# Batch 0 of a gated attention and mixer kernel: z loaded as f32, doubled on VectorE and turned on TensorE

## The chip, the cores and the metric

The kernel runs on one core of a Trainium2 chip. The metric is the device time in microseconds (us) of one execution; the median of several executions is compared. A core has five engines with a queue of instructions each: TensorE (PE in the profile, its weight loads PEld), VectorE (DVE), ScalarE (ACT), GpSimd (POOL) and SyncE (SP). DMA transfers are issued from POOL's queue and from SP's queue here. An instruction that waits holds up everything behind it in its own queue.

## The reference

Two layers, one behind the other, over 8 batches of 3008 rows. The inputs u and v are 8 x 3008 x 256, z is 8 x 3008 x 64, all f32.

```python
scores = (1.0 / S) * np.matmul(z, z.transpose(0, 2, 1))
attn = np.maximum(scores, 0.0) ** 2
x = u * np.matmul(attn, v)                       # gated attention
xt = x.transpose(0, 2, 1)
h = np.maximum(xt @ w_tok1, 0.0) @ w_tok2        # 3008 -> 256 -> 3008
y = x + h.transpose(0, 2, 1)
h2 = np.maximum(y @ w_ch1, 0.0) @ w_ch2          # 256 -> 1536 -> 256
return y + h2
```

## The kernel before

Rows are taken in 24 tiles of 128 (the last has 64 rows, held twice, in both halves of the partitions), four tiles to a **group** of 512 keys. A batch has six rows of groups, one for each block q of 512 queries, and in each row six groups g of 512 keys. `groups` (L179) lists all 288 in the order in which they are worked on; `key_order` (L165) gives the keys of the first row as 0, 5, 1, 2, 3, 4. In batch 0 every group is computed directly; in later batches the ones below the diagonal come from transposing those above it by DMA (`fl`, L213 to L216).

The program's order is written by hand. The loop at L452 takes the groups one by one, and in each: the fetches that `at_group` (L405) has put at this group's number; then `scores` of the group one ahead; then `av` of this group, in two halves of 128 channels; between the halves, from batch 1 on, pieces of the mixer of the batch before (`mix`, L442).

- `scores` (L182): four matmuls with 64 rows of contraction on zT, two at a time in the two halves of the array. For this z is held twice, side by side, so that its transpose fills 128 partitions. They write two PSUM tiles of two banks each (tag `ps`, three buffers for everything that uses the tag). ACT takes each through a scaled ReLU to `rl` (L204), DVE squares it into `at` (L208, L210).
- `av` (L222): eight matmuls on v and `at` into two accumulators of one bank each (tags `acc0`, `acc1`, one buffer each).
- `gate` (L260): at the end of a row of groups DVE multiplies an accumulator by uT into `xT` (L270, L275); after the second one a DMA transpose on SP makes `x` for the mixer (L279).

The steps around the change: `load_z` (L80) loads z on POOL and converts it to bf16 in the DMA (tag `zs`); `turn_z` (L90) doubles it to `zr` (tag `zr`, two buffers) with a copy on the engine that it is given, and transposes it by DMA on SP into zT (L95). `load_v` (L98) loads v on POOL, with conversion. `load_uT` (L108) loads u on POOL with conversion (tag `ur`, two buffers; L111, L114) and right behind it in the program transposes it by DMA on SP (L116; tag `uT`, three buffers). `load_w_tok1`, `load_w_tok2` (its staging tile has tag `ws`, one buffer) and `load_w_ch` bring the weights on POOL.

Before the loop (L393 to L400) the kernel asks, key group by key group, for z and v of batch 0, and after the third for uT(0, 0). Then it doubles and turns the first z with DVE (L439) and computes its scores. In the first five passes of the loop the z of the next group is doubled on DVE and turned on SP (L457 to L459), right ahead of its scores. uT(0, 1) is asked for at group 4, later ones two rows of groups ahead, at the third group of a row (L413). The z of later batches is doubled on POOL (L424).

Of the kernel before, what the change touches and what calls it, by code (L numbers as in the profile page):

```python
# [6 lines left out]

F32 = mybir.dt.float32
BF16 = mybir.dt.bfloat16
# [3 lines left out]
P = 128  # L13
QW = 512
GK = 4
# [12 lines left out]
def kernel(  # L28
# [11 lines left out]
    nc = tc.nc  # L40
    B, S, D = u.shape
    d_qk = z.shape[-1]
# [3 lines left out]
    TAIL = S - (KT - 1) * P  # L46
# [4 lines left out]
    NQ = (S + QW - 1) // QW  # L51
    NG = KT // GK
# [3 lines left out]
    consts = ctx.enter_context(tc.tile_pool(name="consts", bufs=1))  # L56
    sb = ctx.enter_context(tc.tile_pool(name="sb", bufs=2))
    psum = ctx.enter_context(tc.tile_pool(name="psum", bufs=2, space=bass.MemoryType.PSUM))
# [3 lines left out]
    w_tok2_sb = consts.tile([P, DT, S], BF16)  # L62
    w_ch1_sb = consts.tile([P, DT, d_ch], BF16)
    w_ch2_sb = consts.tile([P, CHT, D], BF16)

# [2 lines left out]
    full_tiles = [w // P for w in widths]  # L70

    def rows_of(ap, c):

        n = full_tiles[c]
        return ap[c * QW:c * QW + n * P, :].rearrange("(p t) d -> p t d", t=n)

    def last_rows(ap):
        return ap[(KT - 1) * P:, :]

    def load_z(b, c):  # L80
        zs = sb.tile([P, GK, d_qk], BF16, tag="zs", name="zs", bufs=6)
        n = full_tiles[c]
        nc.gpsimd.dma_start(out=zs[:, :n, :], in_=rows_of(z[b], c))
        if n < GK:
            for r in range(2):
                nc.gpsimd.dma_start(
                    out=zs[r * TAIL:(r + 1) * TAIL, n, :], in_=last_rows(z[b]))
        return zs

    def turn_z(zs, zT, c, engine):  # L90


        zr = sb.tile([P, GK, 2, d_qk], BF16, tag="zr", name="zr", bufs=2)
        engine.tensor_copy(zr[:], zs.unsqueeze(2).to_broadcast([P, GK, 2, d_qk]))  # L94
        nc.sync.dma_start_transpose(  # L95
            out=zT[:, c * GK:c * GK + GK, :], in_=zr.rearrange("p t h d -> p (t h d)"))

    def load_v(b, c):  # L98
        vt = sb.tile([P, GK, D], BF16, tag="v", name="v_sb", bufs=8)
        n = full_tiles[c]  # L100
        nc.gpsimd.dma_start(out=vt[:, :n, :], in_=rows_of(v[b], c))  # L101
        if n < GK:
            for r in range(2):
                nc.gpsimd.dma_start(
                    out=vt[r * TAIL:(r + 1) * TAIL, n, :], in_=last_rows(v[b]))
        vs[b, c] = vt

    def load_uT(b, q):  # L108
        ur = sb.tile([P, QW // P, D], BF16, tag="ur", name="ur", bufs=2)
        n = full_tiles[q]  # L110
        nc.gpsimd.dma_start(out=ur[:, :n, :], in_=rows_of(u[b], q))  # L111
        if n < QW // P:
            nc.gpsimd.memset(ur[TAIL:, n, :], 0.0)
            nc.gpsimd.dma_start(out=ur[:TAIL, n, :], in_=last_rows(u[b]))  # L114
        uT = sb.tile([P, QW // P, DT, P], BF16, tag="uT", name="uT", bufs=3)
        nc.sync.dma_start_transpose(  # L116
            out=uT.rearrange("p t h s -> p (t h) s"),
            in_=ur.rearrange("p t d -> p (t d)"))
        uTs[b, q] = uT
# [35 lines left out]

    zTs, vs, uTs, xTs, xs = {}, {}, {}, {}, {}
    attn = {}

    def direct_block(b, q, g):

        return b == 0 or g >= q

    def key_order(b, q):  # L165
        direct = [g for g in range(NG) if direct_block(b, q, g)]
        if q == 0:
            return [direct[0], direct[-1]] + direct[1:-1]
        direct = [direct[-1]] + direct[:-1]
        flipped = [g for g in range(NG) if not direct_block(b, q, g)]  # L170
        order = []
        while direct or flipped:
            if direct:
                order.append(direct.pop(0))
            if flipped:
                order.append(flipped.pop(0))
        return order

    groups = [(b, q, g) for b in range(B) for q in range(NQ) for g in key_order(b, q)]  # L179
    directs = [t for t in groups if direct_block(*t)]  # L180

    def scores(b, q, g):  # L182
        zT = zTs[b].rearrange("p t s -> p (t s)")
        W = widths[q]
        pss = []
        for pr in range(GK // 2):
            sc = psum.tile([P, 2, QW], F32, tag="ps", name="sc", bufs=3)
            for r in range(2):
                k = g * GK + pr * 2 + r
                h = slice(r * d_qk, (r + 1) * d_qk)  # L190
                nc.tensor.matmul(  # L191
                    sc[:, r, :W], zT[h, k * P:(k + 1) * P], zT[h, q * QW:q * QW + W],
                    start=True, stop=True)
            pss.append(sc)
        at = sb.tile([P, GK * QW], BF16, tag="at", name="at", bufs=3)
        flip = g > q and b > 0
        if flip:

            a4 = at.rearrange("p (j i s) -> p j i s", i=GK, s=P)
        else:  # L200
            a3 = at.rearrange("p (i w) -> p i w", w=QW)
        for pr, sc in enumerate(pss):
            rl = sb.tile([P, 2, QW], BF16, tag="rl", name="rl", bufs=3)
            nc.scalar.activation(rl[:, :, :W], sc[:, :, :W], ACT.Relu, scale=inv_S)  # L204
            pair = slice(2 * pr, 2 * pr + 2)
            if flip:
                r4 = rl.rearrange("p i (j s) -> p j i s", s=P)
                nc.vector.tensor_mul(a4[:, :, pair, :], r4, r4)  # L208
            else:
                nc.vector.tensor_mul(a3[:, pair, :W], rl[:, :, :W], rl[:, :, :W])  # L210
        if flip:
            attn[b, q, g] = a4.rearrange("p j i s -> p i j s")
            fl = sb.tile([P, GK, QW], BF16, tag="fl", name="fl", bufs=10)  # L213
            nc.sync.dma_start_transpose(
                out=fl.rearrange("p j (i s) -> p (j i) s", s=P), in_=at[:])
            attn[b, g, q] = fl[:, :, :]  # L216
        else:
            attn[b, q, g] = a3
# [171 lines left out]
    def new_zT(b):  # L390
        zTs[b] = sb.tile([P, KT, P], BF16, tag="zT", name="zT", bufs=2)

    vorder = key_order(0, 0)  # L393
    new_zT(0)
    zs0 = {}
    for j, c in enumerate(vorder):
        zs0[c] = load_z(0, c)
        load_v(0, c)
        if j == 2:
            load_uT(0, 0)  # L400


    fetch = {}
# [1 line left out]
    def at_group(n, f):  # L405
        fetch.setdefault(n, []).append(f)

    for b in range(B):
        base = b * NQ * NG
        for q in range(NQ):  # L410
            m = b * NQ + q + 2
            if m < B * NQ:
                at_group(base + q * NG + 2, lambda m=m: load_uT(m // NQ, m % NQ))  # L413
        if b + 1 < B:
            held = {}

            def ask_z(b, c, held):
                held[c] = load_z(b + 1, c)

            at_group(base + 3 * NG, lambda b=b: new_zT(b + 1))  # L420
            for j, c in enumerate(vorder):
                at_group(base + 3 * NG + j, lambda b=b, c=c, h=held: ask_z(b, c, h))
                at_group(base + 3 * NG + j + 3, lambda b=b, c=c, h=held:
                         turn_z(h.pop(c), zTs[b + 1], c, nc.gpsimd))  # L424
                at_group(base + (NQ - 1) * NG - 2 + (j if j > 1 else 0),
                         lambda b=b, c=c: load_v(b + 1, c))
    at_group(4, lambda: load_uT(0, 1))
    for c in range(NG):
        at_group(NG + 1 + 4 * c, lambda c=c: load_w_tok1(c))
        at_group(NG + 3 + 4 * c, lambda c=c: load_w_tok2(c))  # L430
# [5 lines left out]
    flat = NQ * NG * 1.73 + NQ * (NQ + 1) / 2 * 0.63  # L436
    budget = 0.0
    ahead = 1
    turn_z(zs0[vorder[0]], zTs[0], vorder[0], nc.vector)  # L439
    scores(*directs[0])  # L440

    def mix(n, left):  # L442
        nonlocal budget
# [8 lines left out]
    for n, (b, q, g) in enumerate(groups):  # L452
        for f in fetch.get(n, []):
            f()
        first, last = n % NG == 0, n % NG == NG - 1
        t = 1.73
        if n + 1 < NG:  # L457
            c = groups[n + 1][2]
            turn_z(zs0[c], zTs[0], c, nc.vector)  # L459
        if direct_block(b, q, g) and ahead < len(directs):  # L460
            scores(*directs[ahead])
            ahead += 1
            t += 0.63
        if b >= 1:
            budget += per_batch * t / flat
        got = budget
        pre, half = av(b, q, g, first, last)
        for f in pre:
            f()
        if not last:  # L470
            half(0)
            mix(n, got / 2)
            half(1)
            mix(n, 0.0)
        else:
            half(0)
            gate(b, q, 0)
            half(1)
            gate(b, q, 1)
            mix(n, 0.0)  # L480
        if q == NQ - 1 and last:
            head, tail = mixer(b, n + 3)
            queue = head + queue + tail
# [32 lines left out]
```

## Time and profile before

| what | value |
|---|---|
| median of 3 runs | 1269.73 us (1267.84 to 1270.58) |
| the profiled execution | 1268.72 us |
| its span, first to last instruction | 1267.0 us |
| mean granted clock of TensorE in it | 0.992 |
| busy: PE, DVE, ACT, POOL | 1192.7, 603.9, 499.9, 147.9 us |

The profile's groups of instructions give line, engine, operation, output and inputs, shapes, then the count, the busy time in us, the mean of one in ns, and behind the second bar the idle time of the engine just before them and what ended it. In the timeline and the chain of waits the first number is the start and the second the duration, both in us from the start of the span. A DMA issue shows on POOL or on SPq, the queue of SyncE; its duration there is that of the issue, not of the transfer.

In the profile's 40 slices of the span, 31.7 us each, the share of PE's time that is busy is a digit in tenths, and so is the granted clock:

```profile
PE   1399999999999999999999999999999999999998
PEclk9799999999999999999999999999999999999999
```

### The profile page before, as it was taken

The page shows a single profiled execution, that of the slowest core. Times are in us where ns is not written, and L with a number is a line of the kernel's source. Part 1 is how long each engine was busy: PE and PEld are TensorE (multiplying, and loading weights), DVE is VectorE, ACT ScalarE, POOL GpSimd, SP SyncE. Part 2 cuts the span into 40 slices and gives each one's busy share as a digit, 9 for nine tenths or more (in the row PEclk, how much of TensorE's full clock was granted, in tenths as well). Part 3 has the DMA queues.
Part 4 walks back from the last instruction along what each step waited for, and adds up shares of the span by engine and source line. Part 5 has one row for each costly group of instructions (what it writes and reads, how often), then busy time and mean ns, then how long its engine had stood idle before and what let it go on. Part 6 is the DMA issues. An engine that isn't in the chain of part 4 may idle for free.

```text
span 1267.0 us, 17239 instructions
## 1 busy us (share of the span) xinstructions
PE 1192.7 (94%) x6986; PEld 623.6 (49%) x7068; DVE 603.9 (48%) x780; ACT 499.9 (39%) x519; POOL 147.9 (12%) x277
## 2 busy tenths in 40 slices
PE   1399999999999999999999999999999999999998
PEld 0133444555455645455455554555455554555565
DVE  1156565444644355534644436543564446444443
ACT  1267644334343144433444343432443334442122
POOL 3323220011101110011200111002110110000000
PEclk9799999999999999999999999999999999999999
DMA  7656995679658697679956797577966788563122
GB/s 112 104 80 95 165 157 117 133 124 177 119 119 144 127 159 125 117 135 154 153 115 109 137 161 138 108 142 132 171 119 129 128 133 155 109 116 83 32 76 65
DMA packets 439487, 157.59 MB, mean 124 GB/s; under 512 B 403504, under 2 KB 417008, under 8 KB 439408
## 3 DMA queue, kind: packets, MB, share of 16 engines
q1 hardware_dynamic: 411040, 123.78, 51.1%
q0 software_dynamic: 28368, 32.72, 18.4%
q8 instruction: 55, 0.90, 0.3%
q14 instruction: 24, 0.20, 0.1%
HBM read 65.40 MB, written 24.64 MB: 71 GB/s over the span
## 4 chain that ended last, share of the span: by engine, by line
PE 83%; DVE 6%; DMA 4%; issue 3%; ACT 2%; POOL 0%; DVEq 0%; ACTq 0%; POOLq 0%
PE acc L244 36%; PE op L351 20%; PE hp L333 17%; PE sc L191 7%; PE a_ps L298 3%; DVE xT L316 3%; ACT rl L204 2%; DMA zT<-zr 2%; DVE h2pre L338 1%; DVE xT L270 1%; DVE at L208 1%; DMA ur<-in_u_dram 1%; DMA fl<-at 1%; DMA uT<-ur 1%; PE h_ps L312 0%
## 5 line engine op out<-in xcount | busy, mean ns | idle before, releaser
L204 ACT ACTIVATE rl<-sc 128x1024 bf16<-128x1024 f32 (+1 forms) x366 | 351.8, 1014 | 424.3 <-PE sc L191 424.3
L244 PE MATMUL acc<-at,v_sb 128*128 128x512 bf16 (+2 forms) x1450 | 361.7, 382 | 14.9 <-DVE xT L270 11.8
L244 PEld LDWEIGHTS <-v_sb 128*128 128x128 bf16 (+1 forms) x2304 | 208.6, 98 | 294.1 <-issue 99.6
L351 PE MATMUL op<-w_ch_sb,h2pre 128*128 128x256 bf16 (+1 forms) x2304 | 279.1, 273 | 1.1
L333 PE MATMUL hp<-xT,w_ch_sb 128*128 128x512 bf16 (+1 forms) x1120 | 272.0, 374 | 2.7 <-DVE xT L316 0.2
L340 ACT ACTIVATE h2pre<-hp 128x1024 bf16<-128x1024 f32 (+1 forms) x144 | 144.9, 1006 | 281.6 <-PE hp L333 263.9
L351 PEld LDWEIGHTS <-h2pre 128*128 128x128 bf16 (+1 forms) x2304 | 224.3, 98 | 62.1 <-ACT h2pre L340 6.3
L208 DVE TENSOR_TENSOR at<-rl 128x1024 bf16<-128x1024 bf16 x210 | 147.7, 705 | 188.3 <-ACT rl L204 188.2
L338 DVE TENSOR_SCALAR h2pre<-hp 128x1024 bf16<-128x1024 f32 (+1 forms) x144 | 172.5, 1200 | 79.3 <-PE hp L333 79.3
L244 PE MATMUL acc<-fl,v_sb 128*128 128x512 bf16 (+1 forms) x805 | 197.3, 370 | 1.8
L333 PEld LDWEIGHTS <-w_ch_sb 128*128 128x128 bf16 x1152 | 112.7, 98 | 131.4 <-issue 4.4
L210 DVE TENSOR_TENSOR at<-rl 128x1024 bf16<-128x1024 bf16 (+1 forms) x156 | 107.7, 699 | 143.1 <-ACT rl L204 139.3
L191 PE MATMUL sc<-zT 64*128 64x512 bf16 (+1 forms) x732 | 114.8, 386 | 47.8 <-DMA zT<-zr 45.7
L359 DVE TENSOR_TENSOR res<-op,u_sb 128x512 f32<-128x512 f32 x88 | 60.6, 689 | 156.3 <-PE op L351 156.3
L270 DVE TENSOR_TENSOR xT<-acc,uT 128x512 bf16<-128x512 f32 (+1 forms) x96 | 61.6, 664 | 62.3 <-PE acc L244 61.8
L94 POOL COPY zr<-zs 128x512 bf16<-128x512 bf16 x42 | 28.8, 685 | 494.6 <-DMA zT<-zr 494.3
L191 PEld LDWEIGHTS <-zT 64*128 64x128 bf16 x732 | 22.2, 94 | 118.1 <-issue 69.5
L316 DVE TENSOR_TENSOR xT<-xT,h_ps 128x1024 bf16<-128x1024 bf16 (+1 forms) x48 | 53.9, 1193 | 19.5 <-PE h_ps L312 19.5
L111 POOL DMA_DIRECT2D ur<-in_u_dram x48 | 25.9, 541 | 246.2 <-DMA uT<-ur 244.1
L312 PE MATMUL h_ps<-w_tok_sb,a_sb 128*128 128x512 bf16 (+1 forms) x191 | 43.4, 374 | 1.7 <-ACT a_sb L304 0.7
L298 PE MATMUL a_ps<-x_sb,w_tok_sb 128*128 128x256 bf16 x384 | 44.4, 273 | 0.0
L101 POOL DMA_DIRECT2D v_sb<-in_v_dram x48 | 26.0, 543 | 144.2 <-PE acc L244 143.4
(25 smaller groups left out, 145.4 us busy)
## 6 DMA issues: line engine op xcount, KB each, us to landing
out_dram<-res SPq DMA_DIRECT2D x88, 256.0 KB, 2.2
v_sb<-in_v_dram POOLq DMA_DIRECT2D x40, 256.0 KB, 4.3
ur<-in_u_dram POOLq DMA_DIRECT2D x40, 256.0 KB, 5.1
zs<-in_z_dram POOLq DMA_DIRECT2D x40, 64.0 KB, 2.9
fl<-at SPq DMA_TRANSPOSE x105, 4.4
v_sb<-in_v_dram POOLq DMA_DIRECT2D x8, 192.0 KB, 5.7
w_ch_sb<-in_moe_w_ch_dram POOLq DMA_DIRECT2D x4, 384.0 KB, 5.8
ur<-in_u_dram POOLq DMA_DIRECT2D x8, 192.0 KB, 3.3
```

What stands on the lines that cost most here:

```text
L191: nc.tensor.matmul(sc[:, r, :W], zT[h, k * P:(k + 1) * P], zT[h, q * QW:q * QW + W], start=True, stop=True)
L204: nc.scalar.activation(rl[:, :, :W], sc[:, :, :W], ACT.Relu, scale=inv_S)
L208: nc.vector.tensor_mul(a4[:, :, pair, :], r4, r4)
L210: nc.vector.tensor_mul(a3[:, pair, :W], rl[:, :, :W], rl[:, :, :W])
L244: nc.tensor.matmul(o, vt[rows, i, dh * P:(dh + 1) * P], rhs, start=st, stop=sp, skip_group_check=True)
L270: nc.vector.tensor_mul(xT[:, dh, :full * P].rearrange("p (t s) -> p t s", s=P), acc[:, :full * P].rearrange("p (t s) -> p t s", s=P), uT[: ...
L298: nc.tensor.matmul(st["a_ps"][:, th, :], w_tok1_sb[:, k, th * P:(th + 1) * P], x[:, :, i, :], start=(k == 0 and th == 0), stop=(k == KT - ...
L316: nc.vector.tensor_add(xT[:, :, :W], xT[:, :, :W], h[:, :, :W])
L333: nc.tensor.matmul(hp[:, r, :W], w_ch1_sb[:, dc, cc * P:(cc + 1) * P], xT[:, dc, :W], start=(dc == 0), stop=(dc == DT - 1))
L338: nc.vector.tensor_single_scalar(h2[:, :, :W], hp[:, :, :W], 0.0, AX.max)
L340: nc.scalar.activation(h2[:, :, :W], hp[:, :, :W], ACT.Relu)
L351: nc.tensor.matmul(op[:rows[i], i, :], st["h2", q, cc // 2][:, cc % 2, c0:c0 + rows[i]], w_ch2_sb[:, cc, :], start=(cc == 0 and i == 0), s ...
```

## The change

For batch 0, z is loaded without conversion, as f32, on SP (`first_z`; its tile shares tag `x`). DVE doubles all six z tiles, with conversion to bf16, before the first scores (`double_z`; the doubled tile shares tag `h2`). The turn is four matmuls against an identity matrix into PSUM (tag `ps`) and a copy on ACT into zT (`turn_first_z`). A z tile is now turned two groups ahead of its use and no longer one. The identity is built on POOL ahead of the v loads, by a memset and a select.

A zero tile of 128x512 (tag `ws`) is filled on DVE, and `fill(n)` runs n matmuls of zeros on it into PSUM: eight ahead of everything, three behind the first turn and two behind the second.

`load_uT` becomes `load_u` and `turn_u`. Both first u loads are asked for right behind the v loads; their turns come at groups 3 and 6, and those of the later ones at the sixth group of a row, three groups behind their loads. z of the later batches is handled as before.

```diff
+    def first_z(c):
+        zf = sb.tile([P, GK, d_qk], F32, tag="x", name="zf", bufs=7)
+        n = full_tiles[c]
+        nc.sync.dma_start(out=zf[:, :n, :], in_=rows_of(z[0], c))
+        if n < GK:
+            for r in range(2):
+                nc.sync.dma_start(
+                    out=zf[r * TAIL:(r + 1) * TAIL, n, :], in_=last_rows(z[0]))
+        return zf
+
+    def double_z(zf):
+        zr = sb.tile([P, GK, 2, d_qk], BF16, tag="h2", name="zr0", bufs=8)
+        nc.vector.tensor_copy(zr[:], zf.unsqueeze(2).to_broadcast([P, GK, 2, d_qk]))
+        return zr
+
+    def turn_first_z(zr, zT, c):
+        zp = psum.tile([P, GK, P], F32, tag="ps", name="zp", bufs=3)
+        for t in range(GK):
+            nc.tensor.matmul(
+                zp[:, t, :], zr[:, t].rearrange("p h d -> p (h d)"), ident[:],
+                start=(t == 0), stop=True, skip_group_check=True)
+        nc.scalar.copy(zT[:, c * GK:c * GK + GK, :], zp[:])
+
+    def fill(n):
+        wp = psum.tile([P, QW], F32, tag="ps", name="wp", bufs=3)
+        for _ in range(n):
+            nc.tensor.matmul(
+                wp[:], zero[:, :P], zero[:], start=True, stop=True, skip_group_check=True)
...
-    def load_uT(b, q):
+    def load_u(b, q):
...
+        urs[b, q] = ur
+
+    def turn_u(b, q):
+        ur = urs.pop((b, q))
         uT = sb.tile([P, QW // P, DT, P], BF16, tag="uT", name="uT", bufs=3)
...
-    zs0 = {}
-    for j, c in enumerate(vorder):
-        zs0[c] = load_z(0, c)
+    zero = sb.tile([P, QW], BF16, tag="ws", name="zero", bufs=1)
+    nc.vector.memset(zero[:], 0.0)
+    make_identity(nc, ident)
+    zf0 = {c: first_z(c) for c in vorder}
+    for c in vorder:
         load_v(0, c)
-        if j == 2:
-            load_uT(0, 0)
+    load_u(0, 0)
+    load_u(0, 1)
...
-                at_group(base + q * NG + 2, lambda m=m: load_uT(m // NQ, m % NQ))
+                at_group(base + q * NG + 2, lambda m=m: load_u(m // NQ, m % NQ))
+                at_group(base + q * NG + 5, lambda m=m: turn_u(m // NQ, m % NQ))
...
-    at_group(4, lambda: load_uT(0, 1))
+    at_group(3, lambda: turn_u(0, 0))
+    at_group(6, lambda: turn_u(0, 1))
...
-    turn_z(zs0[vorder[0]], zTs[0], vorder[0], nc.vector)
+    fill(8)
+    zr0 = {c: double_z(zf0[c]) for c in vorder}
+    turn_first_z(zr0[vorder[0]], zTs[0], vorder[0])
+    fill(3)
     scores(*directs[0])
+    turn_first_z(zr0[vorder[1]], zTs[0], vorder[1])
+    fill(2)
...
-        if n + 1 < NG:
-            c = groups[n + 1][2]
-            turn_z(zs0[c], zTs[0], c, nc.vector)
+        if n + 2 < NG:
+            turn_first_z(zr0[vorder[n + 2]], zTs[0], vorder[n + 2])
```

More of the change, by code (lines that the diff above doesn't have):

```diff
@@ L6 @@
 from concourse._compat import with_exitstack
+from concourse.masks import make_identity
 F32 = mybir.dt.float32
@@ L64 @@
     w_ch2_sb = consts.tile([P, CHT, D], BF16)
+    ident = consts.tile([P, P], BF16)
     full_tiles = [w // P for w in widths]
@@ L153, in load_w_ch @@
                 in_=moe_w_ch2.rearrange("(cc c) d -> c cc d", c=P)[:, c0:c0 + h, :])
-    zTs, vs, uTs, xTs, xs = {}, {}, {}, {}, {}
+    zTs, vs, urs, uTs, xTs, xs = {}, {}, {}, {}, {}, {}
     attn = {}
```

## The prediction

> **What bounds the kernel now.** I read first the table of stretches, which gives each engine's busy time by stretch (columns: stretch, length, then PE, PEld, DVE, ACT, POOL busy, granted clock, DMA share, GB/s).
>
> ```profile
> 0.00:10.00 10.00, 0.00 (x0) 0.00 (x0) 0.43 (x1) 1.28 (x1) 8.38 (x20) 1.00 0.73 94
> 10.00:20.00 10.00, 0.00 (x0) 0.00 (x0) 0.00 (x0) 0.00 (x0) 1.56 (x3) 1.00 1.15 172
> 50.00:60.00 10.00, 3.94 (x11) 1.17 (x12) 1.59 (x3) 1.94 (x2) 3.02 (x5) 0.67 0.89 136
> 400.00:800.00 400.00, 393.43 (x2323) 208.09 (x2348) 195.88 (x251) 157.81 (x165) 47.61 (x90) 1.00 0.78 137
> ```
>
> From the middle on TensorE is busy 98% of the time (393.43 of 400 us), and little is to be had there. In the first 20 us it does nothing, and at 50 to 60 us it works 3.94 of 10. So the end is set by when TensorE begins in earnest, plus a dense remainder. Next I read the waits of the first 70 us, the chain that ended last, and the timeline, for what holds the start.
>
> ```profile
> PE sc L191 <- DMA zT<-zr: 45.7, 6, 21.8
> ```
> ```profile
> 7.05 6.68 DMA ur<-in_u_dram
> 13.75 7.53 DMA uT<-ur
> 25.32 2.47 DMA zT<-zr
> 45.84 5.93 DMA zT<-zr
> ```
> ```profile
> 0.74 1.28 ACT L204 ACT_TABLE_LOAD   x1 [0.74 <-PEq L500]
> 1.23 0.67 POOL L83 DMA_DIRECT2D zs<-in_z_dram  x1 [0.78 <-POOLq L500]
> 3.70 0.43 DVE L94 COPY zr<-zs 128x512 bf16<-128x512 bf16 x1 [3.70 <-DMA zs<-in_z_dram]
> 15.21 11.37 SPq L95 DMA_TRANSPOSE zT<-zr  x2
> 21.78 1.03 PE L191 MATMUL sc<-zT 64*128 64x512 bf16 x4 [21.78 <-DMA zT<-zr]
> 62.07 3.60 PE L244 MATMUL acc<-at,v_sb 128*128 128x512 bf16 x8
> 65.59 0.63 PE L191 MATMUL sc<-zT 64*128 64x512 bf16 x4
> 66.16 1.90 PE L244 MATMUL acc<-at,v_sb 128*128 128x512 bf16 x8
> 68.63 1.28 DVE L270 TENSOR_TENSOR xT<-acc,uT 128x512 bf16<-128x512 f32 x2
> ```
>
> The scores wait 45.7 us in six waits, all for the DMA transpose of z. The first z is there at 3.70 and doubled at 4.13, but its transpose is issued only at 15.21: on SP's queue the transpose of u stands ahead of it, and that waits for u's load until 13.73. Later z transposes take 2.4 to 5.9 us from issue to landing, one per group, each asked for only one group ahead. The sixth group's attention matmuls (its av) begin at 66.16; I call that moment the **anchor**, because TensorE is dense behind it.
>
> **The change part by part.** I sum when the anchor comes afterwards. The profiled run took 1268.72 us, 1.7 more than its 1267.0 span; it lies 1.0 under the median of 1269.73.
>
> *Transposes of z leave the DMA queue.* Six L95 transposes of batch 0 go, and with them the 45.7 us wait. What is late next is built up from the first instructions, with these prices (rows grouped by line and shape; then one SP issue, and landing times of DMAs):
>
> ```profile
> L204 ACT ACTIVATE rl<-sc 128x1024 bf16<-128x1024 f32 x340 | 329.4, 1021 | 420.6 <-PE sc L191 420.6
> L210 DVE TENSOR_TENSOR at<-rl 128x1024 bf16<-128x1024 bf16 x130 | 91.4, 713 | 119.9 <-ACT rl L204 116.2 <-DMA fl<-at 3.7
> L359 DVE TENSOR_TENSOR res<-op,u_sb 128x512 f32<-128x512 f32 x88 | 60.6, 689 | 156.3 <-PE op L351 156.3
> L94 DVE COPY zr<-zs 128x512 bf16<-128x512 bf16 x6 | 1.9, 311 | 3.7 <-DMA zs<-in_z_dram 3.7
> L304 ACT ACTIVATE a_sb<-a_ps 128x512 bf16<-128x512 f32 x8 | 4.8, 597 | 51.7 <-PE a_ps L298 51.7
> L267 POOL MEMSET xT<- 128x128 bf16 x8 | 1.8, 223 | 47.1 <-PE hp L333 47.1
> L94 POOL COPY zr<-zs 128x512 bf16<-128x512 bf16 x42 | 28.8, 685 | 494.6 <-DMA zT<-zr 494.3
> L101 POOL DMA_DIRECT2D v_sb<-in_v_dram x48 | 26.0, 543 | 144.2 <-PE acc L244 143.4
> ```
> ```profile
> 1260.78 0.34 SPq L363 DMA_DIRECT2D out_dram<-res  x1
> ```
> ```profile
> out_dram<-res SPq DMA_DIRECT2D x88, 256.0 KB, 2.2
> ```
>
> 1. *Zero tile and eight leading matmuls.* Engines start their own work at about 1.0 (0.74 and 1.23 above). A zero fill of 128x512 isn't in the trace: it lies between 0.3 (copy) and 0.7 (f32 add); I take 0.5, so 1.5. Eight 512-column matmuls took 3.60 us at half the clock: TensorE is free at 5.0.
> 2. *First z.* One SP issue 0.34 and a landing of 2.2 give 3.6; the doubling, from f32 now, lies between 0.31 and 0.69; I take 0.5: 4.1. This hides behind the eight matmuls; should it come past 5.0, each later us costs one.
> 3. *Identity.* A POOL memset (0.22) and a select that isn't in the trace, between that and a POOL copy (0.69); 1.0 for both with their hand-offs. It is ready at 2.2, before T(0) at 5.0, so it costs only a later first v issue.
> 4. *Turn of z0 on TensorE.* Four 128-column matmuls are not in the trace; between 0.1 (a quarter of a quarter of 1.90) and 1.0 (four scores matmuls cold): 0.5. The ACT copy is priced by the 128x512 row, 0.6. Three more fillers lie between and end at about 6.5. Scores of z0 start there; their first ACT pass starts some 0.55 later, and two passes take 1.94: done at 9.0.
> 5. *Steady groups.* ACT now does 0.6 + 1.94 = 2.54 per group, where TensorE needs turn 0.3, scores and av 2.4. The PSUM ring still has three slots and now serves three users per group, so a turn's copy stands between two groups' passes on ACT. Following it out: ACT ends the passes of the six groups at 9.0, 12.2, 15.1, 17.6, 20.5, 22.7 (the last has no turn), and each av starts 0.75 later (one DVE multiply), the first one at 10.3 behind the second scores. The sixth would start at 23.4, and the scores ahead of it end at 23.6. I add 0.9 for hand-offs I have not listed: **anchor at 24.5**, between 21 and 30.
>
> *Do the loads keep up?* The z loads grow from bf16 to f32 (0.79 MB in place of 0.39 written), on SP; the v loads stay on POOL, 8 issues of 0.543, where 8 z issues leave the line. At the 172 GB/s of the second row, z and v (0.79 + 1.54 MB) are in by 2.5 + 13.5 = 16, and the sixth av wants its v at 24.5. All six doublings stand on DVE ahead of the first multiply, at 9.0, so the last z must be in by about 8.5: it is in at 7.1 if z goes alone (0.79 MB at 172), at 11.6 if it has half the traffic. That is 0 to +2.6, and I take 0, since SP's first z has a lead on v of about 1 us and the 172 counts the written half of converted loads.
>
> The Trainium skill, DMA: Bandwidth & Descriptors, section "Queues, rings and completion order", says that an engine takes packets from its queues in turn. By that z would have about half of the traffic and the sum would be up to 2.6 us higher; that no row here shows z on SP beside v on POOL leaves it to the run.
>
> *u loads apart from their transposes.* On SP the first turn of u has only z loads ahead of it. ur has two buffers, so the third u load, asked for at group 2, waits on POOL for the first turn; queued behind it are weights, z of batch 1 and v of batch 1, all wanted after the first batch: nothing. Likewise the first w_tok2 load waits for the zero tile's buffer, free at about 9, and the f32 z and doubled z tiles sit in buffers (of x and h2) that nothing else wants before the first gate. Ready: u(0,0) lands at 16 + 1.5 = 17.5, and the turn takes 2.4 to 7.5, so 20 to 25. The gate wanted it 2.5 us behind the anchor (68.63 after 66.16), so at 27.0: hidden, with 2 us to spare at the slow end. Without that cover it costs what it is late by, on TensorE, since the accumulators have one buffer each. The third u turn now stands on SP ahead of the second and behind its own load; the second is wanted only at the end of the second row of groups, some 15 us later: nothing.
>
> *Behind the anchor.* The stream of work is unchanged, so it starts 66.16 - 24.5 = 41.7 earlier and ends so: 1268.7 - 41.7 = 1227.0. With the 1.0 that the median lies above this run: **1228 us**.
>
> **The rivals.**
>
> *Half the clock (9%).* TensorE may not come to full clock in the first row of groups, since its turns, scores and av come with short gaps. In the run before, clock and gaps went thus:
>
> ```profile
> 40.00:42.00 2.00, 0.00 (x0) 0.00 (x0) 0.00 (x0) 0.00 (x0) 0.13 (x1) 0.50 0.86 153
> 64.00:66.00 2.00, 2.00 (x8) 0.43 (x6) 0.41 (x1) 0.00 (x0) 0.92 (x2) 0.58 0.88 170
> 66.00:68.00 2.00, 2.00 (x14) 0.71 (x10) 0.69 (x1) 1.94 (x2) 0.00 (x0) 1.00 1.07 159
> ```
>
> After idle stretches of 5 us it is at 0.50, and after some 4 us of work (61.1 to 65.6) at 1.00. At half clock a group takes scores 1.03 + av 3.60 + turn 0.5 = 5.1, so the anchor comes at 10.3 + 5 x 5.1 = 36: 1268.7 - 30 + 1 = 1240. Against it: the gaps I find are under 1 us. The Trainium skill, TensorE: Matmul & The Clock Gate, section "A second HAM failure mode: psum-queue depth-cycling", tells of such a kernel, whose short idles between PSUM turns threw the clock back; by that this rival holds. The row of 66 to 68, with the same three-slot ring, doesn't agree: it is at 1.00.
>
> *u late (10%).* Loads take turns with z, u(0,0) lands at 20 to 22, its turn takes 7.5 and ends at 28 to 30: 1 to 3 us over 27.0, 5 if z's share also delays v. 1229 to 1233.
>
> *Transfers set the second batch (slower, 3%; partly, 4%).* The weights, v and z of batch 1 must come in less time. The DMA shares of the 10 us rows from 0 to 140 sum to 9.5, that is 95 us of transfers (sampled here):
>
> ```profile
> 90.00:100.00 10.00, 9.61 (x49) 3.35 (x49) 6.06 (x10) 8.26 (x9) 0.00 (x0) 1.00 0.01 2
> 150.00:160.00 10.00, 10.00 (x74) 6.33 (x72) 2.83 (x5) 4.38 (x6) 0.53 (x1) 1.00 1.22 205
> ```
>
> The time for them falls from 140 to 98 us. At the 1.22 of the last row they need 78 us and fit; if they run no faster than their mean of 0.68, they need all 140, nothing is won, and z's extra 0.39 MB (2 us at 200 GB/s) and the identity (1 us) come on top: 1268.7 + 3 + 1 = 1273, slower. It decides from a mean share of 0.97 (95 in 98 us); a mean between gives part back, 1240 to 1265. Against it: in the row of 90 to 100 the queues stand empty (0.01) beside a busy TensorE, so order and not rate held them.
>
> *The start moves and the end doesn't (2%).* The stretch behind the anchor absorbs it all in new waits: 1270, no change. TensorE's 98% speaks against it.
>
> **How the numbers follow.** The forecast with its own bounds (anchor 21 to 30: 1224 to 1234, and 1222 if start and hand-offs are as short as single rows) has 72%. 1222 to 1240 takes in the late u and the half clock: 91%. I take 1221 to 1240. A difference of 0.2%, 2.5 us, is about what a measurement of this kernel can tell from no change. Faster: 72 + 9 + 10 + 4 = 95%; same 2%; slower 3%.
>
> **What would show it.** In the changed profile: the wait of scores for zT's DMA gone; scores from about 6.5; granted clock 1.00 by 10; the sixth av at 21 to 30; the first gate without a wait for uT; from there on the same durations as behind 66.16. I am wrong if the last doubling comes past 9.5, if av matmuls stay at 0.44 us, if the gate waits for uT, or if TensorE is idle for transfers between 60 and 110.

## The result, and the profile after

The changed kernel takes 1232.54 us (1230.74 to 1234.13, 4 runs) against 1268.93 us before (4 runs): a ratio of 0.971, with a 95% interval of 0.969 to 0.973. The forecast was 1228; the gain is 36.4 us where 41.7 were forecast. (The forecast started from a median of 1269.73 over three runs; a fourth brought it down by 0.8.)

The profiled execution took 1232.48 us, with a span of 1230.7. These are rows of its timeline (start, duration, instruction, and in brackets the idle time in front of it and what ended it):

```profile
2.91 0.50 DVE L113 CAST zr<-zf 128x512 bf16<-128x512 f32 x1 [1.78 <-DMA zf<-in_z_dram]
5.89 0.61 PE L229 MATMUL sc<-zT 64*128 64x512 bf16 x4
7.02 0.43 DVE L113 CAST zr<-zf 128x512 bf16<-128x512 f32 x1 [3.60 <-DMA zf<-in_z_dram]
12.96 0.43 DVE L113 CAST zr<-zf 128x512 bf16<-128x512 f32 x1 [1.25 <-DMA zf<-in_z_dram]
13.31 2.53 DVE L248 TENSOR_TENSOR at<-rl 128x1024 bf16<-128x1024 bf16 x4
14.04 2.29 PE L282 MATMUL acc<-at,v_sb 128*128 128x512 bf16 x5 [4.64 <-DVE at L248]
28.60 1.90 PE L282 MATMUL acc<-at,v_sb 128*128 128x512 bf16 x8
31.07 1.28 DVE L308 TENSOR_TENSOR xT<-acc,uT 128x512 bf16<-128x512 f32 x2
```

The scores of the first z stand at 5.89, where they stood at 21.78. The anchor, the sixth av, stands at 28.60, where it stood at 66.16: 37.6 us earlier. One long gap is left: the first av waits 4.64 us for the squaring, which stands on DVE behind the sixth doubling, and that waits for the last z. The rows of the granted clock (last but two of each row; two us each) show what else the gap did:

```profile
8.00:10.00 2.00, 1.33 (x10) 0.43 (x9) 0.70 (x2) 1.91 (x4) 0.00 (x0) 1.00 1.08 225
12.00:14.00 2.00, 0.00 (x0) 0.00 (x0) 1.04 (x3) 0.00 (x0) 0.00 (x0) 0.50 1.14 214
20.00:22.00 2.00, 2.00 (x15) 0.88 (x14) 1.06 (x2) 1.73 (x3) 0.55 (x2) 1.00 0.45 78
```

TensorE is at full clock, falls to half in the gap and comes back by 20; the first av takes 3.57 us for its eight matmuls.

Of the 37.6 us at the anchor, 36.3 reach the end of the span. To see where 1.3 went I divide each profiled span at starts of gates (the first DVE product of xT at the end of a row of groups): the first gate of batch 0, its last, the first and the second of batch 1. Each number is the length of a piece in us.

| kernel | to first gate | to last gate of batch 0 | to first gate of batch 1 | to its second gate | rest of the span |
|---|---|---|---|---|---|
| before | 68.6 | 76.1 | 20.2 | 36.4 | 1065.7 |
| after | 31.1 | 76.4 | 21.6 | 36.1 | 1065.5 |

The rest is the same to 0.2 us. The 1.4 us are lost between the last gate of batch 0 and the first of batch 1. There the timeline of the changed kernel has this (first DVE, then TensorE; the third row is what SP's queue waited for between 50 and 150: how long in all, how often, and the longest):

```profile
125.38 1.29 DVE L246 TENSOR_TENSOR at<-rl 128x1024 bf16<-128x1024 bf16 x2 [2.27 <-DMA fl<-at]
```
```profile
126.13 2.06 PE L282 MATMUL acc<-at,v_sb 128*128 128x512 bf16 x8 [0.93 <-DVE at L246]
```
```profile
SPq L154 <- DMA ur<-in_u_dram: 15.5, 1, 15.5
```

A squaring waits for its buffer, which an attention transpose on SP's queue still has to read. That queue stood 15.5 us at a turn of u, until its load had come. In the kernel before, the same queue waited 13.0 us for a u load at this place too, but up to the first gate of batch 1 no squaring there waited for an attention transpose, and no av for a squaring:

```profile
SPq L116 <- DMA ur<-in_u_dram: 15.8, 2, 13.0
161.02 0.69 DVE L208 TENSOR_TENSOR at<-rl 128x1024 bf16<-128x1024 bf16 x1 [0.60 <-ACT rl L204]
```

That the 15.5 us at the turn are the cause of the 1.4 us is argued from these rows. The 1.4 us are also less than the 3.4 us by which the four times of this kernel differ, and each profile is one execution.

### The profile page after: what moved, and what is told of

It reads as the page before. It is cut to its first block, busy times and chain, and to the rows that moved or that the text cites. A ratio compares the mean times of both kernels' runs of the same rounds, so it can differ in the third digit from the quotient of the medians.

```text
span 1230.7 us, 17401 instructions
## 1 busy us (share of the span) xinstructions
PE 1198.9 (97%) x7105; PEld 626.3 (51%) x7105; DVE 603.6 (49%) x781; ACT 503.1 (41%) x525; POOL 142.5 (12%) x271
## 4 chain that ended last, share of the span: by engine, by line
PE 85%; DVE 7%; issue 3%; ACT 3%; DMA 1%; SPq 0%; DVEq 0%; ACTq 0%
PE acc L282 36%; PE op L389 20%; PE hp L371 18%; PE sc L229 6%; PE a_ps L336 3%; DVE xT L354 3%; ACT rl L242 2%; DVE h2pre L376 1%; DVE xT L308 1%; DVE at L248 1%; DVE at L246 1%; DMA fl<-at 1%; DMA zf<-in_z_dram 1%; PE h_ps L350 1%; ACT h2pre L378 1%
## 5 line engine op out<-in xcount | busy, mean ns | idle before, releaser
L282 PE MATMUL acc<-at,v_sb 128*128 128x512 bf16 (+3 forms) x1464 | 359.7, 379 | 19.8 <-DVE xT L308 12.1
L371 PE MATMUL hp<-xT,w_ch_sb 128*128 128x512 bf16 (+1 forms) x1152 | 274.8, 374 | 1.3 <-DVE xT L354 0.2
L282 PE MATMUL acc<-fl,v_sb 128*128 128x512 bf16 (+1 forms) x840 | 200.3, 370 | 0.0
```

The lines of the kernel that those rows point to most:

```text
L282: nc.tensor.matmul(o, vt[rows, i, dh * P:(dh + 1) * P], rhs, start=st, stop=sp, skip_group_check=True)
L371: nc.tensor.matmul(hp[:, r, :W], w_ch1_sb[:, dc, cc * P:(cc + 1) * P], xT[:, dc, :W], start=(dc == 0), stop=(dc == DT - 1))
```

## The experiments

All runs change the changed kernel, except where the kernel before is named. Profiled spans are cut as above in the table at the end of this part. Each row of that table is one execution; times and ratios come from four, unless one is named.

**Doublings late.** What held the first av: DVE's order, or the loads?

```diff
-    zr0 = {c: double_z(zf0[c]) for c in vorder}
-    turn_first_z(zr0[vorder[0]], zTs[0], vorder[0])
+    turn_first_z(double_z(zf0[vorder[0]]), zTs[0], vorder[0])
...
-    turn_first_z(zr0[vorder[1]], zTs[0], vorder[1])
+    turn_first_z(double_z(zf0[vorder[1]]), zTs[0], vorder[1])
...
-            turn_first_z(zr0[vorder[n + 2]], zTs[0], vorder[n + 2])
+            turn_first_z(double_z(zf0[vorder[n + 2]]), zTs[0], vorder[n + 2])
```

> Only the place of the doublings on VectorE differs from the changed kernel: each stands right ahead of its own turn, no longer all six ahead of the first squaring. Theory A (the first squaring waited for the last z only because of VectorE's order): the first av starts at 9 to 10 in place of 14.04, at full clock, and the sixth av (28.60 in the changed kernel) at 22.3 to 23.5; the time is 5 to 6 us below the changed kernel's. Theory B (the loads themselves set the pace, v or z): the sixth av stays at 27 or later, with waits on the v or z DMAs, and the time falls by at most 1.5 us.

1231.48 us (1229.67 to 1232.83), ratio to the kernel before 0.971 (0.969 to 0.973), as the changed kernel. The first half of theory A held, nearly (the first av came at 10.74, expected at 9 to 10); the second didn't. Theory B's late sixth av and small gain came, but TensorE waited for the doublings and not for the loads:

```profile
8.65 0.75 DVE L113 CAST zr<-zf 128x512 bf16<-128x512 f32 x2
10.74 1.90 PE L282 MATMUL acc<-at,v_sb 128*128 128x512 bf16 x8
13.76 0.40 PE L120 MATMUL zp<-ident,zr 128*128 128x128 bf16 x4 [1.12 <-DVE zr L113]
17.74 0.40 PE L120 MATMUL zp<-ident,zr 128*128 128x128 bf16 x4 [1.43 <-DVE zr L113]
21.72 0.40 PE L120 MATMUL zp<-ident,zr 128*128 128x128 bf16 x4 [1.21 <-DVE zr L113]
27.33 1.90 PE L282 MATMUL acc<-at,v_sb 128*128 128x512 bf16 x8
```

The first av runs at 10.74 and at full clock (1.90). But now each doubling stands behind the squarings of the group before, so doubling, turn, copy, scores, ReLU and squaring run one after the other: a turn every 3.98 us where the changed kernel, once started, has one every 2.6 to 3.0. The sixth av comes only 1.3 us earlier. The u turns of this run are the changed kernel's, and yet the piece ahead of batch 1 takes 20.2 us (table below), as before the change: the place of these turns alone doesn't make the 1.4 us. One thing that differs: the last u load ahead of batch 1 goes out on POOL at 104.21, in the changed kernel at 106.13. Taking a wait away at the head of a queue made a new one inside the loop.

**No leading matmuls**, once in the changed kernel and once with the doublings late (one execution each).

```diff
-    fill(8)
...
-    fill(3)
...
-    fill(2)
```

> The changed kernel without the 13 matmuls on the zero tile. Theory A: TensorE idles from 9.4 to 14.0 anyway and its clock falls back to half, so the leading matmuls buy nothing: sixth av at 28.3 to 29.0, same time within 0.5 us. Rival (they buy the clock of the first row of groups): scores and av stay at half clock longer, sixth av at 31 or later.

> Doublings late as in the first experiment, and no leading matmuls. Theory A: now that the wait at 9.4 to 14.0 is gone, the leading matmuls matter: the first two av run at half clock, sixth av 1 to 2.5 us later than with doublings late alone (24 to 25.5). Rival (they never matter): sixth av within 0.5 us of it, or earlier by up to 1 since the first turn needn't wait for them.

Sixth av at 28.27 and 27.03, against 28.60 and 27.33 with them; times 1231.88 and 1229.89. For the changed kernel theory A holds: the matmuls on zeros gave the first scores full clock (0.61 us; without them 1.04), but a clock that is lost again in the gap buys nothing. With the doublings late the rival holds: the first av runs at half clock in part (2.84 us for eight), yet the next z comes later than TensorE does.

**z on two queues.** Every second z load is issued from ACT's queue.

```diff
+        eng = nc.sync if vorder.index(c) % 2 == 0 else nc.scalar
...
-        nc.sync.dma_start(out=zf[:, :n, :], in_=rows_of(z[0], c))
+        eng.dma_start(out=zf[:, :n, :], in_=rows_of(z[0], c))
...
-                nc.sync.dma_start(
+                eng.dma_start(
```

> The changed kernel with every second f32 z load issued from ScalarE's queue in place of SyncE's. If z and v packets take turns queue by queue, z gets two turns in three: the last z lands at 9.5 to 11 in place of 12.96, the first av starts as much earlier, sixth av at 25.5 to 27. If the bytes in front of z set it, whatever the queue: last z at 12.5 to 13.5, sixth av at 28 to 29.

The first case: the last z is doubled from 9.93, the first av starts at 11.01 after a gap of 1.25 us, and the sixth at 23.48, earlier than the 25.5 to 27 expected, since the clock held this time (eight matmuls in 2.06 us).

```profile
9.93 0.43 DVE L114 CAST zr<-zf 128x512 bf16<-128x512 f32 x1 [0.27 <-DMA zf<-in_z_dram]
11.01 2.06 PE L283 MATMUL acc<-at,v_sb 128*128 128x512 bf16 x8 [1.25 <-DVE at L249]
23.48 1.90 PE L283 MATMUL acc<-at,v_sb 128*128 128x512 bf16 x8
```

And yet the one execution took 1233.49. The first gate is 5.1 us earlier, and 6.4 us more than in the changed kernel are lost ahead of the first gate of batch 1 (28.0 us there, 21.6 in the changed kernel, 20.2 in the kernel before). Now the mixer's first matmuls wait for x, whose transposes stand on SP behind the same turn of u (timeline of SP's queue, then waits of TensorE between 50 and 180, then of SP's queue between 50 and 150):

```profile
94.55 4.63 SPq L318 DMA_TRANSPOSE x_sb<-xT  x1
113.21 1.23 SPq L155 DMA_TRANSPOSE uT<-ur  x1
114.54 2.43 SPq L318 DMA_TRANSPOSE x_sb<-xT  x1
```
```profile
PE a_ps L337 <- DMA x_sb<-xT: 4.6, 1, 4.6
```
```profile
SPq L155 <- DMA ur<-in_u_dram: 15.4, 2, 13.9
```

The load that this turn waits for is asked for on POOL in two parts, at 106.21 and 107.91, behind a wait of 8.2 us for a w_tok2 tile and behind loads of v; the gate at which x is finished starts at 102.1.

**Each half of the change alone.** The kernel before with the u loads apart, and nothing else; and the changed kernel with `load_uT` as it was.

```diff
-        if j == 2:
-            load_uT(0, 0)
+    load_u(0, 0)
+    load_u(0, 1)
...
+                at_group(base + q * NG + 5, lambda m=m: turn_u(m // NQ, m % NQ))
```

> The kernel before with only the u loads taken apart from their transposes; z of batch 0 by converting loads and DMA transposes, as before. Theory A (the wait for u ahead of z on SyncE's queue was one part, the six serial z transposes the larger one): first scores at 8 to 11 in place of 21.78, sixth av at 48 to 56 in place of 66.16, time 1251 to 1259. Rival (the queue order was the whole trouble): sixth av below 38, time below 1242.

> The changed kernel with the u loads and transposes together as in the kernel before. Theory A: z's way is what counts in the first row of groups, sixth av at 28 to 30; and the 1.2 us that the changed kernel gave back between the first and the second batch come from its later u turns on SyncE's queue, so from the sixth av to the end this one takes 1 us less: 1201 in place of 1202.1 from the sixth av to the last instruction. Rival: the u split carries a share of the start: sixth av later than 31 or a first gate that waits for uT. Second rival: the give-back has nothing to do with u's turns and stays.

With the u split alone: 1253.30 us, ratio 0.987 (0.986 to 0.989). The first scores stand at 10.27, the sixth av at 50.06, as theory A expected, and TensorE still waits for z transposes, 29.3 us in six waits:

```profile
10.27 1.04 PE L195 MATMUL sc<-zT 64*128 64x512 bf16 x4 [10.27 <-DMA zT<-zr]
19.67 1.03 PE L195 MATMUL sc<-zT 64*128 64x512 bf16 x4 [8.36 <-DMA zT<-zr]
50.06 1.90 PE L248 MATMUL acc<-at,v_sb 128*128 128x512 bf16 x8
```

So the order on SP's queue alone was worth 16 us; the new way of z takes out the other 20. (The two halves don't add: with z off SP's queue u has nothing left to hold up at the start.) The parts of z's way were not taken apart: no run kept the DMA transposes and asked for all six at the start, so how much of the 20 us is their own time and how much their late issue stays open.

With z alone: 1232.12 us, ratio 0.971 (0.970 to 0.972), the same as the changed kernel. Sixth av at 28.78, first gate at once behind it; from the sixth av to the end 1200.7 us, where the changed kernel has 1202.1. The piece ahead of batch 1 is back to 20.2. That is what theory A expected, in one profile; the 1 us doesn't show in the times, and the run with doublings late lost nothing in that piece with the later turns in place. So that these turns cost the 1 us is not shown.

**Turns of u later still**, three groups, to let x and attention transposes go first on SP; and with it both earlier changes.

```diff
-                at_group(base + q * NG + 5, lambda m=m: turn_u(m // NQ, m % NQ))
+                at_group(base + q * NG + 8, lambda m=m: turn_u(m // NQ, m % NQ))
```

> The changed kernel with the later u turns three groups later still (at the third group of the next row). Theory A (at the batch boundary a u turn waits for its load on SyncE's queue and holds up the x and attention transposes behind it): the 0.9 us wait of av for the squaring at 126 goes, from the sixth av to the end 1201 us, time 1 us below the changed kernel's. Rival: the wait stays, time within 0.3 us.

> Doublings late, z on two queues and u turns three groups later, together. Theory A: sixth av at 22 to 23.5 (z is no longer late, so the two queues add nothing to the late doublings), 1201 us from there to the end: 1225 to 1227, against 1232.5 for the changed kernel. Theory B: 1230 or more.

Both came out slower than the changed kernel: 1239.86 us (0.978, 0.976 to 0.979) and 1238.74 us (0.977, 0.975 to 0.979). The second's first gate is at 29.8, as with doublings late alone (its sixth av was expected at 22 to 23.5): z on two queues adds nothing there. The reason for the loss stands in the waits of POOL: a u load needs a buffer that a turn has to empty, and that turn now stands on SP (33.74) behind the x transpose of the first row of groups (32.41). The row below names a squaring, and not the turn, as what came last, so the link is read from the order of the program:

```profile
37.57 0.53 POOL L145 DMA_DIRECT2D ur<-in_u_dram  x1 [17.23 <-DVE at L248]
```

The same load went out at 28.67 in the changed kernel. All weights queue behind it, and the last u load ahead of batch 1 goes out at 111.65, in the changed kernel at 106.13. I had weighed what the turn holds up on SP and not who waits for the turn on POOL.

**Relief for POOL's queue.** Theory C gives the u turns back to their loads, C' a second staging buffer to w_tok2 (`bufs=2` for tag `ws`); then both, and both without the leading matmuls. All four have z on two queues.

```diff
-                at_group(base + q * NG + 2, lambda m=m: load_u(m // NQ, m % NQ))
-                at_group(base + q * NG + 5, lambda m=m: turn_u(m // NQ, m % NQ))
+                at_group(base + q * NG + 2, lambda m=m: load_uT(m // NQ, m % NQ))
...
-        st = sb.tile([P, DT, QW], BF16, tag="ws", name="ws", bufs=1)
+        st = sb.tile([P, DT, QW], BF16, tag="ws", name="ws", bufs=2)
```

> z loads on two queues, and the u loads and transposes together again as in the kernel before. The run with two queues began its first gate 5.1 us earlier than the changed kernel (25.95 to 31.07) and lost 6.4 us more at the end of the first batch, where a u turn on SyncE's queue waited 13.9 us for its load and held up the x transposes. Theory C (GpSimd's queue falls behind because its loads wait for u turns that stand three groups late, and so the last u load of the first batch comes too late): first gate at 25.9 to 26.5, from it to the end 1198.3 as in the run with z alone, span 1224 to 1225. Rival D (the bytes of the first batch don't fit into the shorter time, whatever the order): from the first gate to the end 1202 to 1206, span 1228 or more.

> z loads on two queues with the changed kernel's u turns, and two staging buffers for w_tok2 in place of one. Theory C' (GpSimd's queue falls behind because each w_tok2 load and its copies hold it for 4 to 9 us): the last u load before the second batch is issued at 100 or earlier in place of 107.9, the loss at the end of the first batch (from its last gate to the first of the second, 28.0 us there, 20.2 without loss) falls to 20.2 to 21, span 1224 to 1225. Rival D (bytes): it stays above 25, span above 1228.

> Both: z on two queues, u loads and transposes together, two staging buffers. Theories C and C': first gate at 25.9 to 26.5, no loss at the end of the first batch (20.2 us from its last gate to the next), span 1224, time 1225 to 1227. Rival D: span 1228 or more.

> As the run with both, without the 13 matmuls on the zero tile. If they buy the clock of the first groups where no wait for the last z stands in front of the av: first gate 1 to 2.5 us later than in that run, and scores of the first groups at 1.03 us. If not: within 0.5 us of it.

Times: 1229.14 (ratio 0.969, 0.967 to 0.971), 1233.50 (0.972, 0.970 to 0.975), 1227.57 (0.968, 0.965 to 0.970) and 1228.70 (0.968, 0.967 to 0.970). The profiled spans in pieces, cut as above:

| kernel | to first gate | to last gate of batch 0 | to first of batch 1 | to its second | second gate of batch 1 at |
|---|---|---|---|---|---|
| before | 68.6 | 76.1 | 20.2 | 36.4 | 201.3 |
| after | 31.1 | 76.4 | 21.6 | 36.1 | 165.2 |
| doublings late | 29.8 | 77.2 | 20.2 | 36.1 | 163.3 |
| no leading matmuls | 30.7 | 76.8 | 21.0 | 36.1 | 164.6 |
| late, no leading matmuls | 29.5 | 76.8 | 20.2 | 36.1 | 162.6 |
| z on two queues | 26.0 | 76.1 | 28.0 | 36.1 | 166.2 |
| u split alone | 52.5 | 76.3 | 20.2 | 36.1 | 185.1 |
| z alone | 31.3 | 76.4 | 20.2 | 36.1 | 163.9 |
| u turns later | 31.1 | 78.6 | 22.7 | 38.0 | 170.4 |
| all three | 29.8 | 76.7 | 28.1 | 37.3 | 171.9 |
| two queues, u together | 27.3 | 76.3 | 20.9 | 40.0 | 164.5 |
| two queues, two staging buffers | 27.0 | 77.0 | 21.6 | 36.1 | 161.6 |
| two queues, both | 25.5 | 76.4 | 20.3 | 39.4 | 161.5 |
| the same, no leading matmuls | 26.6 | 76.1 | 20.2 | 38.2 | 161.1 |

In every profile 1065.5 to 1065.7 us follow the second gate of batch 1. Theories C and C' held for the piece they were made for: from 28.0 it falls to between 20.2 and 21.6. For the whole they didn't. In the profile of the first run (the slowest of its four executions, 2.8 us above the median) the first gate came at 27.3 (25.9 to 26.5 expected), 1202.8 us followed it, and the span was 1230.1, all as rival D had it; the other spans of 1226.8 to 1227.2 lie between the theories (1224 to 1225, and 1228 or more). The second staging buffer alone brings no time: its four executions have a median of 1233.50, and the one profiled is the fastest of them, 4.5 us below.

Where the u turns are back, the next piece takes 38.2 to 40.0 in place of 36.1. There, in the run with both, SP's queue has only attention transposes from 116.35 to 130.5; a squaring waits for its buffer because the attention transposes in front are still on their way, and the mixer behind it (waits between 120 and 165; DMA share last but one):

```profile
DVE at L245 <- DMA fl<-at: 5.6, 1, 5.6
PE h_ps L347 <- DVE xT L351: 2.8, 1, 2.8
```
```profile
110.00:120.00 10.00, 10.00 (x67) 5.27 (x65) 2.77 (x4) 4.87 (x6) 1.15 (x3) 1.00 1.08 184
120.00:130.00 10.00, 7.59 (x34) 2.96 (x34) 3.41 (x6) 3.38 (x4) 1.48 (x3) 1.00 1.13 155
```

So in the profiles a start that is 5.6 us earlier at the first gate (25.5 for 31.1) is worth 3.6 us at the second gate of batch 1, and none of them passes it before 161. A wall at 161 is not shown: the fastest execution of the run with both has a span of 1223.9, and if 1065.6 us follow there too, it passes at 158 (an estimate). Nor do the DMA shares above 1 settle it for rival D: the run with z alone has 1.25 and 1.12 in the same two rows and loses nothing in either piece. Whether the bytes of the transfers or their order on SP and POOL set the loss stays open: no run took transfers out. The run with both reliefs and z on two queues is the fastest, 4 to 5 us below the changed kernel, but the intervals of the two ratios overlap by a hair (up to 0.9696, and from 0.9694).

The last run answers for the matmuls on zeros. Without them the first scores take 1.03 us and the first gate comes 1.1 us later, as expected if they buy the clock of the first groups; the second gate of batch 1 comes 0.4 us earlier all the same, and the times don't tell the two apart.

## Why the prediction was right, and where it was off

The range and the direction held; the forecast was 4.5 us too low, and two steps explain it: 4.1 us at the anchor (28.60 for 24.5) and 1.3 us behind it, less the 0.8 by which the median of the kernel before came down.

- *Mechanism.* The wait of scores for z's transposes (45.7 us) is gone and the work behind the second gate of batch 1 is the same to 0.2 us. The runs of each half agree: with z's way alone the whole gain is there. That a gain at the anchor runs through to the end was right but for 1.3 us.
- *Steps 1 to 4.* Each came out within 0.15 us of its price or below it: leading matmuls from 1.19, TensorE free at 4.58 (5.0 forecast), the first doubling at 2.91 (3.6), its length 0.50 (0.5), four turn matmuls 0.63 (0.5), the copy 0.59 (0.6), first scores 5.89 (6.5). The lower bound for the turn was mis-worked: four 128-column matmuls are half of the eight in 1.90 us at a quarter of their columns, 0.24 and not 0.1. They took 0.40 at full clock.
- *Step 5.* Once started, the last four av of the first row began 2.4 to 2.6 us apart (21.27, 23.86, 26.23, 28.60); the forecast had 2.2 to 3.2 from ACT's passes. The pace was near, but ACT didn't set it: TensorE was busy without a break from 16 to 30, and ACT waited for it (0.27 us before the pass at 26.12). The two sums had lain close together (2.54 us for ACT, 2.7 for TensorE).
- *"Do the loads keep up?"* **This term was mis-sized.** I took 0 of a range of 0 to +2.6, with the last z in at 8.5 or before and 11.6 at the most. It came at 12.9, outside that range, and the last doubling at 12.96 is past the 9.5 that I had named as a sign of being wrong. The first av, which would have followed the scores at 9.4, started at 14.04, and, as the clock fell in the gap, took 3.57 us in place of 1.90: 4.6 + 1.7 us, where the early start and the unused hand-off allowance give back some 2. That the anchor stayed in its own range of 21 to 30 is in part luck: these gains have nothing to do with the loads. The rate was about as forecast (186 GB/s for 172); what failed is z's share of it. The queues between 1 and 13 us (packets, MB, share of the engines' time):

```profile
q0 software_dynamic: 949, 1.45, 75.1%
q1 hardware_dynamic: 1024, 0.79, 24.4%
```

 The z queue (q1) and the queue of v and u (q0) moved about as many packets, but z got 35% of the bytes (0.79 of 2.24 MB) and a quarter of the DMA engines' time. The rule of the Trainium skill that I weighed (DMA: Bandwidth & Descriptors, "Queues, rings and completion order": turns queue by queue, packet by packet) was the better guide, and these packet counts agree with it; I read "turn" as half the bytes. With z on two queues the last one came 3.0 us earlier. Between 4 and 7 us of that run the three queues moved 139, 170 and 197 packets, the last number v's, near to one turn each. Up to 1.5 us of the 3.0 can come from the earlier issue: the last z issue was done at 4.92 on SP alone, and at 3.47 on the two queues.
- *Half the clock.* The clock did fall, in the gap of 4.64 us, and was back by 20; from there on it stayed at 1.00, so the three-slot ring alone doesn't bring it down. But in other runs it fell behind shorter gaps too. Take the four runs with z on two queues, doublings ahead and leading matmuls: the first av stood behind gaps of 1.25, 1.32, 1.38 and 1.66 us. Behind the two shorter ones its eight matmuls took 2.06 us, behind the longer ones 3.23 and 3.32, and the granted clock of 12 to 14 was 0.50 (the runs with two staging buffers, then with both):

```profile
10.40 3.23 PE L283 MATMUL acc<-at,v_sb 128*128 128x512 bf16 x8 [1.38 <-DVE at L249]
10.57 2.06 PE L279 MATMUL acc<-at,v_sb 128*128 128x512 bf16 x8 [1.32 <-DVE at L245]
```

 That is 1.2 us in the first av alone; the first gate came at 26.96 in the one, at 25.51 in the other. The length of one gap doesn't decide it: with doublings late a gap of 2.88 us left the next turn at full clock (0.40 us). What does decide is not shown. The argument against this rival, that the gaps are under 1 us, failed at the start (1.00 and 4.64 us); from 20 to 140 the longest gap is 1.1 us, and the clock is at 1.00. The rule of the Trainium skill on short idles between PSUM turns (TensorE: Matmul & The Clock Gate, "A second HAM failure mode: psum-queue depth-cycling") agrees with these two runs only in that short idles threw the clock back. It happened once and not again and again, and the idles were waits for z and the squaring.
- *u late.* The first turn was issued at 15.77 and done by 19.5; the gate at 31.07 didn't wait. Right, and with more room than forecast.
- *"POOL's third u load waits: nothing".* At the start nothing, as forecast. At the batch boundary more came of it. The rival "transfers set the second batch, partly" came true in a small way, for 1.3 us in the changed kernel, and for 8 us in the profile with z on two queues. I summed transfers against time (95 us in 98) and took the fit for safety. In the profiles with z on two queues the order on POOL moved that piece: with the last u load asked for at 102.35 in place of 107.91 (two staging buffers), the loss against the kernel before fell from 7.8 to 1.4 us.

## What to carry to other kernels

A load that shares the DMA engines with another queue need not get half of them: z, with small packets beside large ones (0.77 KB against 1.5 KB written, by the two rows above), got as many packets as its neighbour, a third of the bytes and a quarter of the time. Here a range for its landing would have been better worked out from packets. Before moving work on an in-order queue, follow both ends: what stands behind it there, and which other queue waits for the buffer that it frees (three groups later on SP cost 7 us by way of POOL). And when a start is pulled forward, the next place where transfers crowd is the first to look at: cutting the span at fixed marks shows in one table what each microsecond of the start is worth there. One profile per kernel is little for this: the executions of one kernel differed by up to 6 us here.

## What the runs showed of the hardware that I had not expected

Matmuls on zeros brought TensorE to full clock as other matmuls do: the first scores took 0.61 us behind them and 1.04 without. In no pair of runs did they change the time clearly (1227.57 with and 1228.70 without, on the fastest kernel). The column of the granted clock doesn't show this: at the start it is 1.00 in the run without them too, between 10 and 12, where eight av matmuls took 3.57 us. There the durations are the better witness.

```profile
5.45 1.03 PE L226 MATMUL sc<-zT 64*128 64x512 bf16 x4 [1.14 <-ACT zT L124]
10.00:12.00 2.00, 1.89 (x5) 0.71 (x5) 1.91 (x4) 1.32 (x2) 0.00 (x0) 1.00 1.12 209
```
